# Loading an expert's rows one expert earlier, and spreading the gate's last steps over many blocks

## The chip, the cores and the metric

The kernel runs on one core of a Trainium2 chip. The core has the matrix engine TensorE (PE), the vector engine VectorE (DVE), ScalarE (ACT), GpSimd (POOL), SyncE (SP), which here mostly issues transfers, and 16 DMA engines. The metric is the device time of one execution in microseconds (us); smaller is better. TensorE runs at a clock that the chip grants: 1.00 in a row is the full 2.4 GHz, 0.50 is 1.2 GHz.

## What is computed

```python
def reference(**kw):
    attn_out = _attn_ref(...)                  # a scan over 768 steps, 4 x 8 heads of 40
    x = attn_out.transpose(0, 2, 1, 3).reshape(3072, 320)
    x = _moe_ref(x, w_gate, w1, w2, capacity)  # N, D, E, F = 3072, 320, 8, 1024
    return _moe2_ref(x, w_in, w_out)           # relu(x @ w_in)**2 @ w_out, width 2048

def _moe_ref(x, w_gate, w1, w2, capacity):
    logits = x @ w_gate
    expert_idx = np.argmax(logits, axis=1)
    gate_w = softmax(logits)[arange(N), expert_idx]
    ...                                        # row i goes to place counts[e] of its expert
    h = np.maximum(np.einsum('ecd,edf->ecf', disp, w1), 0.0)
    y = np.einsum('ecf,efd->ecd', h, w2)
    out[i] = gate_w[i] * y[expert_idx[i], pos[i]]   # for rows that had a place, else 0
```

All products are float32. The kernel splits an operand into a high part (rounded to TensorE's fp32r) and a low part (the rest) and adds three products: high by high, high by low, low by high.

## The kernel before

The program has three stages, one behind the other: the attention scan, which also computes the gate and scatters each token's row into a table of rows `zs_s` in memory; the **expert stage**, eight experts in an order that the gate decides at run time (largest count first); and the dense layer at the end ("moe2", tiles with a `g` at the end of their names), in six groups. The order of instructions on every engine is that of the code: the stage runs under a manual schedule, and nothing is reordered.

**An expert** has up to 480, 480, 480, 448, 416, 400, 384 and 384 rows in the order of experts. Its hidden width of 1024 is cut into eight **blocks** f = 0 to 7 (`Ffn.run`). A block does this, in this order:

- `first(f)`: 8 matmuls into `phe` (L1369), then ScalarE makes the high part of the activated block, `hhe` (L1373), and VectorE the low part, `hle` (L1374);
- `second(f-2)`: the block from two blocks earlier (`DEPTH = 2`) is multiplied into the outputs `poe`, three matmuls for each tile of rows (L1393 to L1395; four tiles of rows, three from expert 6 on). The third reads `hle`;
- `between(f)`, the work that is not the product itself. All of it is issued behind `second(f-2)`, and so VectorE meets it between the `hle` of this block and that of the next.

What `between` holds: **rows turned** at f = 2, 4 and 6 (4, 5, 6 for expert 0), each time a third of the next expert's rows, transposed by TensorE into `pte` (L1249) and split by ScalarE and VectorE (L1231, L1232, L1236, L1237); **weights** (`prep`), at each block the slices for a block up to four ahead, split by ScalarE (L1186, L1188, L1190), GpSimd (L1187) and VectorE (L1189, L1191), with a load of two slices by SP (L1165 to L1168); **`conv.step`**, which converts a piece of moe2's weights and stores it to memory (load L1090, ScalarE L1106, GpSimd L1107, VectorE L1108 to L1114, store L1115), at every block of experts 0 to 6 but the first four, and from expert 2 on but f = 4 and 6.

Three more pieces of the gate's arithmetic stand in it, each at one place: the rest of `gate.order` (24 short VectorE instructions) at f = 7 of expert 5; `gate.final` (the places of all tokens in the table, 30 VectorE instructions and a small matmul into `pfin`, L1030) at f = 7 of expert 6; and `places`, which makes one-hot matrices `oh` that put the last expert's rows straight into the first group of moe2, at f = 0 (two diagonals `Dslot`, `Dgate`, L1302, and some constants), f = 3 (three `oh`, L1316) and f = 5 (three pairs of L1322 and L1323) of expert 7.

The **row load** (L1491, `xs`, one DMA of 100 to 128 partitions, up to 1280 floats each) is issued by SP at the start of each expert, for the expert after it. Ahead of it SP reads that expert's number from `oat_i` into a register (L1448). `xs` has two buffers, and the rows of the running expert were turned in the expert before.

```python
                    nxt = load_next(e + 1) if e + 1 < NE else None      # before the blocks of e
                    ...
                        turns = (2, 4, 6) if e else (4, 5, 6)           # in between(f)
                        if f == turns[0] and nxt is not None:
                            st["x"] = F.xT(f"e{e + 1}", nxt)
                        if f in turns and nxt is not None:
                            next(st["x"])
```

Of the kernel before, what the change touches and what calls it, by code (L numbers as in the profile page):

```python
# [806 lines left out]
class Gate:  # L807
# [174 lines left out]
    def order(self, pool):  # L982
# [28 lines left out]
        for b in range(3):  # L1011
            V.memset(self.before[32 * b : 32 * b + 1, 32 * b + 32 :], 1.0)
        for i in range(n):
            V.memset(slots[:, i : i + 1], float(SLOTS[i + 1]))
            V.memset(base[:, i : i + 1], float(FROM[i + 1]))
        V.memset(self.base[:, 0:1], 0.0)
        V.memset(self.size[:, 0:1], float(SLOTS[0]))
# [4 lines left out]
        yield  # L1022

    def final(self, pool, ps):
        V, s2 = self.nc.vector, [128, NC]

        def t(shape, nm):
            return pool.tile(shape, F32, name=nm, bufs=1)

        self.nc.tensor.matmul(ps[:, 0:8], self.before, self.cntb, start=True, stop=True)  # L1030
        off = t([128, 8], "off")
        V.tensor_copy(off, ps[:, 0:8])
        q, pos, keep, big, a, b, bk, nb = (
            t([128, NC, 8] if n == "fq" else s2, n) for n in ("fq", "pos", "keep", "big", "fa", "fb", "bk", "nb"))
        V.tensor_tensor(q, self.oh, off.unsqueeze(1).to_broadcast([128, NC, 8]), ALU.mult)
        V.tensor_reduce(pos, q, axis=AX.X, op=ALU.add)
        V.tensor_tensor(pos, self.lp, pos, ALU.add)
        V.tensor_scalar(keep, pos, float(self.cap) - 0.5, None, ALU.is_lt)
        V.tensor_tensor(self.gate, self.gate, keep, ALU.mult)
        def of_token(z, out):  # L1040
            V.tensor_tensor(q, self.oh, z.unsqueeze(1).to_broadcast([128, NC, 8]), ALU.mult)
            V.tensor_reduce(out, q, axis=AX.X, op=ALU.add)

        of_token(self.size, big)
        V.tensor_tensor(big, self.ar, big, ALU.is_ge)
        of_token(self.base, a)
        V.tensor_tensor(a, a, self.ar, ALU.add)
        V.scalar_tensor_tensor(b, self.ei, float(self.capp), pos, ALU.mult, ALU.add)
        V.tensor_tensor(bk, big, keep, ALU.mult)
        V.tensor_scalar(nb, bk, -65536.0, 65536.0, ALU.mult, ALU.add)  # L1050
        V.tensor_tensor(nb, nb, b, ALU.add)
        V.tensor_copy(self.idxo, nb)

        V.tensor_scalar(nb, b, float(NE * NS1) - 0.5, float(FROM[NE]), ALU.is_gt, ALU.mult)
        V.tensor_tensor(b, b, nb, ALU.add)
        V.tensor_tensor(b, b, bk, ALU.mult)
        V.tensor_scalar(nb, big, -1.0, 1.0, ALU.mult, ALU.add)
        V.tensor_scalar_add(a, a, float(NE * NS1))
        V.tensor_tensor(a, a, nb, ALU.mult)
        self.slot = t([128, 4], "slot")  # L1060
        V.tensor_scalar_add(self.slot, a[:, 0:4], -float(NE * NS1 + FROM[NE - 1]))
        V.tensor_tensor(a, a, b, ALU.add)
        V.tensor_copy(self.idx, a)
        mc = t([128, 1], "mc")
        V.tensor_tensor(off, self.carA, self.size, ALU.subtract)
        V.tensor_reduce(mc, off, axis=AX.X, op=ALU.max)
        V.tensor_scalar(mc, mc, 0.5, None, ALU.is_gt)
        V.tensor_copy(self.ovf, mc)

# [124 lines left out]
class Ffn:  # L1194
# [90 lines left out]
    def places(self, slot, gate, nb, bs):  # L1285
# [24 lines left out]
        Ds, Dg = diag("slot", slot), diag("gate", gate)  # L1310
# [7 lines left out]
        yield  # L1318
# [5 lines left out]
        yield  # L1324
# [95 lines left out]
def tile_kernel(tc, cap, E, VN, VR, R0, R1, wg, w1, w2, wi, wo, out):  # L1420
# [32 lines left out]
    with ExitStack() as es0:  # L1453
# [26 lines left out]
        with ExitStack() as es:  # L1480
# [13 lines left out]
            def block(e):  # L1494
                return SLOTS[e] // -(-SLOTS[e] // 128)
# [49 lines left out]
            with tc.manual_schedule():  # L1545
                LEAD, done = 4, [4]

                def prep(s):

                    for _ in range(2):  # L1550
                        i = done[0]
                        if i > s + LEAD or i >= len(W):
                            break
                        if i % 2 == 0 and i >= 6:
                            W.load(i + 4, F.raw(f"rw{i + 4}"), 2)
                        W.prep(i)
                        done[0] += 1
# [8 lines left out]
                for i in range(3):  # L1566
                    conv.load(i)
                for e in range(NE):
                    X = F.X
                    F.busy = True  # L1570
                    nxt = load_next(e + 1) if e + 1 < NE else None
# [3 lines left out]
                    def between(f):  # L1575
                        turns = (2, 4, 6) if e else (4, 5, 6)
                        if f == turns[0] and nxt is not None:
                            st["x"] = F.xT(f"e{e + 1}", nxt)
# [5 lines left out]
                        if e == NE - 3 and f == 7:  # L1584
                            next(order)
                        if e == NE - 2 and f == 7:
                            gate.final(F.dp, F.ppt.tile([128, 512], F32, tag="t", name="pfin"))
                        if e == NE - 1:
                            if f == 0:
                                st["p"] = F.places(gate.slot, gate.gate, ns // bs, bs)  # L1590
# [4 lines left out]
                            if f in (0, 3, 5):  # L1595
                                next(st["p"])
# [9 lines left out]

                F.turn("g0", st["g"])
# [98 lines left out]
```

## Time and profile before

| | |
|---|---|
| median of 3 runs | 1069.04 us (1067.66 to 1071.59) |
| the profiled execution | 1070.31 us |
| its span, first to last instruction | 1068.60 us |
| mean granted clock over the span | 0.929 |
| TensorE busy (matmuls) | 952.2 us, 89% |
| VectorE busy | 689.8 us, 65% |
| ScalarE, GpSimd busy | 574.1 us, 341.7 us |
| the expert stage, from the trace | about 457 to 693 us |

Busy time is the time in which an engine executes an instruction. An engine carries out its instructions in the order written, so one that waits holds up everything behind it. The time outside the span (1070.31 - 1068.60 = 1.71 us) is start and end.

### The profile page before, as it was taken

To read this page: it belongs to the slowest core of one execution; us is meant where nothing else is said; L and a number is where in the kernel's file an instruction comes from. 1 tells how busy PE (TensorE), PEld (TensorE's weight loads), DVE (VectorE), ACT (ScalarE), POOL (GpSimd) and SP (SyncE) were. 2 spreads that over 40 slices of the span, in tenths; PEclk is the share of its full clock that TensorE was granted. 3 is DMA by queue.
4 is the path that set the end of the run, shared out by engine and by line. 5 is a ranking of instruction groups with operands and counts; after the bars stand their busy time and mean duration, and the time that the engine had idled before them with its cause. 6 is when DMAs were issued, how large, how long until landed. Compare 5 with 4: busy or idle time off the path is not lost.

```text
span 1068.6 us, 33405 instructions
## 1 busy us (share of the span) xinstructions
PE 952.2 (89%) x13866; PEld 865.0 (81%) x13866; DVE 689.8 (65%) x1407; ACT 574.1 (54%) x1344; POOL 341.7 (32%) x531
## 2 busy tenths in 40 slices
PE   5477887988879899998899999899999999999995
PEld 3366877877778788788799998788999999999995
DVE  6869678696776845568888888957434344444432
ACT  8245676766568688155556556456444443434331
POOL 5452454564554121126555555423201010000000
PEclk7587898988989899699899999999999999999998
DMA  7555665546543342267756776422200000000000
GB/s 185 128 139 168 187 190 170 150 142 177 145 124 99 94 118 78 86 185 217 222 166 217 227 231 205 140 75 78 62 14 25 25 26 25 1 25 1 25 1 29
DMA packets 80659, 122.89 MB, mean 115 GB/s; under 512 B 9679, under 2 KB 57409, under 8 KB 79561
## 3 DMA queue, kind: packets, MB, share of 16 engines
q1 hardware_dynamic: 71173, 100.09, 31.8%
q10 hardware_dynamic: 7020, 12.78, 4.2%
q0 software_dynamic: 2304, 7.78, 2.3%
q8 instruction: 111, 1.82, 0.7%
q14 instruction: 51, 0.42, 0.1%
HBM read 91.36 MB, written 29.35 MB: 113 GB/s over the span
## 4 chain that ended last, share of the span: by engine, by line
PE 61%; DVE 15%; DMA 7%; ACT 7%; issue 6%; POOL 2%; SPq 0%; ACTq 0%; DVEq 0%; POOLq 0%
PE phg L1369 14%; PE phe L1369 6%; PE pog L1395 5%; PE pog L1394 5%; PE pog L1393 5%; PE px L430 4%; PE pq L518 3%; DVE pr L287 2%; PE poe L1395 2%; DMA xs<-zs_s 2%; DMA wB<-in_E_dram 2%; PE poe L1393 2%; PE poe L1394 2%; PE pu L444 2%; PE py L540 1%
## 5 line engine op out<-in xcount | busy, mean ns | idle before, releaser
L1379 DVE SCALAR_TENSOR_TENSOR sqg<-phg,rg 128x512 f32<-128x512 f32 x96 | 66.3, 691 | 119.0 <-ACT rg L1378 119.0
L1378 ACT ACTIVATE rg<-phg 128x512 f32<-128x512 f32 x96 | 57.3, 596 | 110.4 <-PE phg L1369 110.2
L1381 DVE TENSOR_TENSOR hlg<-sqg,hhg 128x512 fp32r<-128x512 f32 x96 | 67.9, 707 | 65.9 <-ACT hhg L1380 63.2
L1380 ACT CAST hhg<-sqg 128x512 fp32r<-128x512 f32 x96 | 59.6, 620 | 79.0 <-DVE sqg L1379 79.0
L1369 PE MATMUL phg<-xhg,e 128*128 128x512 f32 x264 | 93.1, 393 | 0.0
L1395 PE MATMUL pog<-e,hlg 128*128 128x320 f32 x240 | 74.2, 309 | 0.0
L1394 PE MATMUL pog<-e,hhg 128*128 128x320 f32 x240 | 74.1, 309 | 0.0
L1393 PE MATMUL pog<-e,hhg 128*128 128x320 f32 x240 | 74.0, 308 | 0.0
L430 PE MATMUL px<-TB,X 128*104 128x128 f32 x384 | 64.7, 338 | 3.5 <-ACT TB L348 1.7
L1187 POOL TENSOR_TENSOR e<-rw,e 128x256 fp32r<-128x256 f32 x51 | 42.6, 840 | 71.0 <-ACT e L1186 60.2
L189 POOL TENSOR_TENSOR e<-e,wB 104x512 f32<-104x512 f32 x40 | 54.0, 1368 | 32.4 <-DVE wB L161 23.3
L430 PEld LDWEIGHTS px<-TB,X 128*104 128x104 f32 x384 | 58.8, 220 | 5.7 <-ACT TB L348 2.5
L189 POOL TENSOR_TENSOR e<-e 104x512 f32<-104x512 f32 x21 | 28.6, 1363 | 108.6 <-DVE e L165 49.0
L1508 POOL DMA_INDIRECT x2g<-zs_s,idx x24 | 23.7, 987 | 113.6 <-ACT hhg L1380 105.7
L1369 PE MATMUL phe<-xhe,e 128*128 128x480 f32 (+4 forms) x176 | 58.6, 374 | 0.0
L1369 PEld LDWEIGHTS phg<-xhg,e 128*128 128x128 f32 x264 | 49.6, 188 | 8.9
L518 PE MATMUL pq<-rq,vut 128*64 128x64 f32 x768 | 48.5, 232 | 8.0 <-ACT vut L509 7.8
L518 PEld LDWEIGHTS pq<-rq,vut 128*64 128x64 f32 x768 | 45.0, 144 | 11.0 <-ACT vut L509 10.6
L449 ACT COPY vu<-pu 32x320 f32<-32x320 f32 x96 | 40.0, 417 | 23.1 <-PE pu L444 21.7
L356 POOL COPY TB<-TT 32x256 f32<-32x256 f32 x92 | 42.6, 463 | 30.4 <-DVE TT L268 14.0
L1395 PE MATMUL poe<-e,hle 128*120 128x320 f32 (+4 forms) x150 | 47.5, 317 | 5.3 <-DVE hle L1374 5.3
L1373 ACT ACTIVATE hhe<-phe 128x480 fp32r<-128x480 f32 (+4 forms) x64 | 33.8, 529 | 34.0 <-PE phe L1369 33.7
(367 smaller groups left out, 2914.4 us busy)
## 6 DMA issues: line engine op xcount, KB each, us to landing
e<-in_E_dram ACTq DMA_DIRECT2D x60, 208.0 KB
rw<-in_w_dram SPq DMA_DIRECT2D x30, 320.0 KB
zs_s<-zt SPq DMA_DIRECT2D x24, 320.0 KB
rw<-in_w_dram SPq DMA_DIRECT2D x30, 256.0 KB
e<-in_E_dram SPq DMA_DIRECT2D x9, 832.0 KB
ru<-in_VR_dram SPq DMA_DIRECT2D x48, 128.0 KB
cr<-in_wi_dram SPq DMA_DIRECT2D x20, 256.0 KB
cr<-in_wo_dram SPq DMA_DIRECT2D x20, 256.0 KB
```

What stands on the lines that cost most here:

```text
L189: eng.tensor_tensor(z, z, f, ALU.mult)
L356: (copy or self.nc.gpsimd.tensor_copy)(self.TB[c % 2][t, :, t], self.TT[t, 8 * (c % 4) : 8 * (c % 4) + 8])
L430: self.nc.tensor.matmul(px[par][0:104, 128 * o : 128 * o + 128], X[:, par, o, :], TB[:, 4 * par + o, :], start=True, stop=True)
L518: T.matmul(pq[s, 64 * q : 64 * q + 64], vut[:, q, s], rt[:, :, q, pp], start=True, stop=True)
L1369: T.matmul(o, lt, rt, start=(i == 0), stop=(i == len(seq) - 1))
L1378: A.activation(r[:, :n], o, AF.Relu)
L1379: V.scalar_tensor_tensor(sq[:, :n], o, 0.0, r[:, :n], ALU.max, ALU.mult)
L1380: A.copy(hh[:, :n], sq[:, :n])
L1381: V.tensor_tensor(hl[:, :n], sq[:, :n], b32(hh)[:, :n], ALU.subtract)
L1393: T.matmul(o, hh[:, t], W["h2"], start=(f == 0), stop=False)
L1394: T.matmul(o, hh[:, t], W["l2"], start=False, stop=False)
L1395: T.matmul(o, hl[:, t], W["h2"], start=False, stop=(f == NF - 1))
```

## The change

Three things are moved; every instruction of before is still issued, and each engine has as many as it had.

1. **The row load** for expert e + 2 is issued at block 4 of expert e. The rows of expert 1 are loaded ahead of the loop, those of expert 2 at block 4 of expert 0.
2. **`gate.order`'s rest and `gate.final`** become one generator of 21 steps. A step of one to three short instructions is taken in each block of experts 2 to 6 in which no rows are turned, and the last is done in block 0 of expert 6.
3. **`places`** becomes a generator of more steps: the constants at block 7 of expert 6; then, in expert 7, `Dslot` at block 0, `Dgate` at 1, one `oh` each at 2, 3 and 4, and one pair for `gs` each at 5, 6 and 7.

```diff
@@ order
             V.memset(self.before[32 * b : 32 * b + 1, 32 * b + 32 :], 1.0)
+        yield
         for i in range(n):
             V.memset(slots[:, i : i + 1], float(SLOTS[i + 1]))
...
             V.tensor_reduce(to[:, 1:NE], cmp, axis=AX.X, op=ALU.add)
-        yield
+            yield
@@ final (a yield behind each one to three of its instructions)
-        self.nc.tensor.matmul(ps[:, 0:8], self.before, self.cntb, start=True, stop=True)
...
+        p = ps()
+        self.nc.tensor.matmul(p[:, 0:8], self.before, self.cntb, start=True, stop=True)
+        V.tensor_copy(off, p[:, 0:8])
+        yield
         V.tensor_tensor(q, self.oh, off.unsqueeze(1).to_broadcast([128, NC, 8]), ALU.mult)
+        yield
         V.tensor_reduce(pos, q, axis=AX.X, op=ALU.add)
+        yield
...
@@ places
-        Ds, Dg = diag("slot", slot), diag("gate", gate)
+        yield
+        Ds = diag("slot", gate.slot)
+        yield
+        Dg = diag("gate", gate.gate)
         yield
...
             self.oh.append(o)
-        yield
+            yield
...
             V.tensor_reduce(self.gs[:, i : i + 1], r, axis=AX.X, op=ALU.add)
-        yield
+            yield
@@ tile_kernel
+                def rest():
+                    yield from order
+                    yield from gate.final(F.dp, lambda: F.ppt.tile([128, 512], F32, tag="t", name="pfin"))
...
+                steps = rest()
+                nl = SLOTS[NE - 1]
+                spots = F.places(gate, -(-nl // 128), block(NE - 1))
+                ahead = {1: load_next(1)}
                 for e in range(NE):
...
-                    nxt = load_next(e + 1) if e + 1 < NE else None
+                    nxt = ahead.pop(e + 1, None)
...
+                        if f == 4 and e + 2 < NE:
+                            ahead[e + 2] = load_next(e + 2)
...
-                        if e == NE - 3 and f == 7:
-                            next(order)
                         if e == NE - 2 and f == 7:
-                            gate.final(F.dp, F.ppt.tile([128, 512], F32, tag="t", name="pfin"))
+                            next(spots)
+                        if 2 <= e < NE - 1 and f not in turns:
+                            next(steps, None)
                         if e == NE - 1:
-                            if f == 0:
-                                st["p"] = F.places(gate.slot, gate.gate, ns // bs, bs)
...
-                            if f in (0, 3, 5):
-                                next(st["p"])
+                            next(spots, None)
```

The order of instructions shows where they stand now. First SP, around the row load for expert 5 (400 rows: `xs` of 100 partitions); `rw` are weights, `cr` and `ct` the pieces of `conv.step`, `obe` the outputs of expert 3. Before, at the start of expert 4:

```order
L1090 DMA cr_10463<-in_wo_dram 128x512
L1115 DMA wof_s<-ct_10378 128x256
L1448 TENSOR_LOAD oat_i
L1448 ISA x2
L1491 ISA
L1491 DMA xs_10483<-zs_s 100x1280
L1165 ISA
L1165 DMA rw_10510<-in_w_dram 128x2x256
...
L1115 DMA wof_s<-ct_10465 128x256
L1402 DMA zs_s<-obe_0_10557 112x320
```

And with the change, in block 4 of expert 3 (the lines of after.py are some 20 higher):

```order
L1109 DMA cr_10333<-in_wo_dram 128x512
L1134 DMA wof_s<-ct_10293 128x256
L1470 TENSOR_LOAD oat_i
L1470 ISA x2
L1513 ISA
L1513 DMA xs_10379<-zs_s 100x1280
L1184 ISA
L1184 DMA rw_10388<-in_w_dram 128x2x256
...
L1134 DMA wof_s<-ct_10335 128x256
```

The load stands behind the conversion's store and ahead of a weight load as it did, half an expert earlier, and the first store behind it is that of the block after.

Next VectorE at the turn from expert 6 to expert 7. Before, all of `final` stands between two low parts:

```order
L1374 SCALAR_TENSOR_TENSOR hle_7_11599<-phe_7_11589,hhe_7_11598 128x384
L1189 TENSOR_TENSOR ws<-rw_11421,ws 64x128
L1191 TENSOR_TENSOR ws<-rw_11421,ws 128x320
L1032 COPY off<-pfin 128x8
L1035 TENSOR_TENSOR fq<-oh,off 128x192
L1036 TENSOR_REDUCE pos<-fq 128x24
L1037 TENSOR_TENSOR pos<-lp,pos 128x24
```

With the change the same instructions stand three experts earlier, one to three in a block:

```order
L1396 SCALAR_TENSOR_TENSOR hle_0_10134<-phe_0_10124,hhe_0_10133 128x448
L1208 TENSOR_TENSOR ws<-rw_9978,ws 64x128
L1210 TENSOR_TENSOR ws<-rw_9978,ws 128x320
L1127 TENSOR_SCALAR ct_10162<-ct_10162 128x256
L1128 SCALAR_TENSOR_TENSOR ct_10162<-cr_10020,ct_10162 128x256
L1132 TENSOR_SCALAR ct_10112<-ct_10112 128x256
L1133 SCALAR_TENSOR_TENSOR ct_10112<-cr_9916,ct_10112 128x256
L1041 COPY off<-pfin 128x8
L1396 SCALAR_TENSOR_TENSOR hle_1_10195<-phe_1_10185,hhe_1_10194 128x448
```

`off` is now made behind the conversion of block 0 of expert 3, and the next `hle` follows it at once.

## Rows read from the trace of the kernel before

**Rows 1.** The page, part 1: VectorE's busy time, share of the span, instructions.

```profile
PE 952.2 (89%) x13866; PEld 865.0 (81%) x13866; DVE 689.8 (65%) x1407; ACT 574.1 (54%) x1344; POOL 341.7 (32%) x531
```

**Rows 2.** Stretches, expert stage: from:to, length, busy (count) per engine, clock, DMA share, GB/s.

```profile
457.00:693.00 236.00, 218.88 (x1296) 207.77 (x1297) 195.74 (x451) 132.53 (x362) 120.48 (x149) 0.98 0.65 201
```

**Rows 3.** Waits of TensorE, 488.06 to 692.50 us: total, times, longest.

```profile
PE pte L1249 <- DMA xs<-zs_s: 11.5, 6, 4.1
PE poe L1395 <- DVE hle L1374: 5.3, 3, 4.6
```

**Rows 4.** Timeline of TensorE: start, length, instruction, [idle before it and its releaser].

```profile
528.57 0.98 PE L1249 MATMUL pte<-ident,xs 112*128 112x112 f32 x4 [4.09 <-DMA xs<-zs_s]
...
590.22 0.53 PE L1249 MATMUL pte<-ident,xs 100*128 100x100 f32 x4 [1.45 <-DMA xs<-zs_s]
...
674.24 0.63 PE L1395 MATMUL poe<-e,hle 128*128 128x320 f32 x1 [4.59 <-DVE hle L1374]
```

**Rows 5.** Stretches behind the two longest waits, and one at rest (PEclk is third from last).

```profile
528.57:534.50 5.93, 5.93 (x20) 5.36 (x21) 3.70 (x9) 3.25 (x9) 2.10 (x3) 0.52 1.03 338
534.50:540.00 5.50, 5.50 (x35) 5.13 (x34) 4.58 (x10) 1.83 (x5) 2.65 (x4) 1.00 0.67 214
674.24:677.50 3.26, 3.26 (x11) 3.26 (x12) 3.08 (x14) 0.00 (x0) 2.65 (x3) 0.50 0.27 71
```

**Rows 6.** Stretches from an expert's first `hle`: experts 1 and 6, and 1 to 6.

```profile
488.06:521.87 33.81, 30.68 (x180) 28.36 (x180) 28.32 (x61) 18.44 (x51) 19.36 (x25) 1.00 0.69 216
...
643.21:673.63 30.42, 24.77 (x153) 23.50 (x151) 27.20 (x76) 16.95 (x50) 14.75 (x18) 1.00 0.66 208
...
488.06:673.63 185.57, 169.12 (x1017) 161.45 (x1016) 155.22 (x365) 105.41 (x290) 99.82 (x124) 0.98 0.68 212
```

**Rows 7.** Waits of VectorE, 488.06 to 673.63 us.

```profile
DVE ct L1108 <- POOL ct L1107: 9.3, 6, 2.2
DVE e L1189 <- ACT e L1188: 3.7, 3, 1.3
DVE ws L1189 <- ACT ws L1188: 3.7, 3, 1.3
DVE xle L1232 <- ACT xhe L1231: 2.9, 4, 0.9
DVE xRle L1237 <- ACT xRhe L1236: 1.5, 1, 1.5
```

**Rows 8.** Timeline of VectorE, 640 to 680 us.

```profile
665.80 0.16 DVE L1032 COPY off<-pfin 128x8 f32<-128x8 f32 x1
...
671.42 0.78 DVE L1057 TENSOR_SCALAR nb<-big 128x24 f32<-128x24 f32 x1
...
673.63 0.55 DVE L1374 SCALAR_TENSOR_TENSOR hle<-phe,hhe 128x384 fp32r<-128x384 f32 x1
...
674.98 0.17 DVE L1291 MEMSET ones<- 128x128 f32 x1
...
676.61 0.86 DVE L1302 TENSOR_SCALAR Dslot<-ident,slot 128x128 f32<-128x128 f32 x4
```

**Rows 9.** Timelines of SP's queue, ScalarE and VectorE, start of expert 4.

```profile
585.03 0.35 SPq L1491 DMA_DIRECT2D xs<-zs_s  x1
...
588.64 0.37 SPq L1115 DMA_DIRECT2D wof_s<-ct  x1
...
593.85 0.43 ACT L1106 ACTIVATE ct<-cr 128x256 f32<-128x256 f32 x1 [1.71 <-DMA wof_s<-ct]
...
595.25 0.29 DVE L1108 TENSOR_SCALAR ct<-ct 128x256 int32<-128x256 int32 x1 [2.17 <-POOL ct L1107]
```

**Rows 10.** Stretches: behind a row load, and around block 4 of the same expert.

```profile
590.00:596.00 6.00, 5.78 (x37) 5.76 (x38) 3.35 (x8) 3.05 (x9) 1.74 (x3) 1.00 0.88 269
602.00:608.00 6.00, 6.00 (x41) 5.95 (x40) 4.78 (x10) 2.83 (x7) 1.58 (x2) 1.00 0.64 209
```

**Rows 11.** A stretch of the attention scan with many short idle times of TensorE.

```profile
294.00:321.00 27.00, 21.48 (x638) 19.49 (x635) 20.27 (x30) 17.75 (x44) 14.69 (x19) 0.87 0.41 127
```

More of the change, by code (lines that the diff above doesn't have):

```diff
@@ L1012, in order @@
             V.memset(self.before[32 * b : 32 * b + 1, 32 * b + 32 :], 1.0)
+        yield
         for i in range(n):
             V.memset(slots[:, i : i + 1], float(SLOTS[i + 1]))
+        V.memset(self.size[:, 0:1], float(SLOTS[0]))
+        yield
+        for i in range(n):
             V.memset(base[:, i : i + 1], float(FROM[i + 1]))
         V.memset(self.base[:, 0:1], 0.0)
-        V.memset(self.size[:, 0:1], float(SLOTS[0]))
+        yield
         for z, to in ((slots, self.size), (base, self.base)):
@@ L1039, in final @@
         V.tensor_tensor(self.gate, self.gate, keep, ALU.mult)
[L1040 to L1044, printed above, removed]
+        yield
+        V.tensor_tensor(q, self.oh, self.size.unsqueeze(1).to_broadcast([128, NC, 8]), ALU.mult)
+        yield
+        V.tensor_reduce(big, q, axis=AX.X, op=ALU.add)
         V.tensor_tensor(big, self.ar, big, ALU.is_ge)
-        of_token(self.base, a)
+        yield
+        V.tensor_tensor(q, self.oh, self.base.unsqueeze(1).to_broadcast([128, NC, 8]), ALU.mult)
+        yield
+        V.tensor_reduce(a, q, axis=AX.X, op=ALU.add)
         V.tensor_tensor(a, a, self.ar, ALU.add)
+        yield
         V.scalar_tensor_tensor(b, self.ei, float(self.capp), pos, ALU.mult, ALU.add)
@@ L1050, in final @@
         V.tensor_scalar(nb, bk, -65536.0, 65536.0, ALU.mult, ALU.add)
+        yield
         V.tensor_tensor(nb, nb, b, ALU.add)
         V.tensor_copy(self.idxo, nb)
+        yield
         V.tensor_scalar(nb, b, float(NE * NS1) - 0.5, float(FROM[NE]), ALU.is_gt, ALU.mult)
         V.tensor_tensor(b, b, nb, ALU.add)
+        yield
         V.tensor_tensor(b, b, bk, ALU.mult)
@@ L1058, in final @@
         V.tensor_scalar_add(a, a, float(NE * NS1))
+        yield
         V.tensor_tensor(a, a, nb, ALU.mult)
-        self.slot = t([128, 4], "slot")
         V.tensor_scalar_add(self.slot, a[:, 0:4], -float(NE * NS1 + FROM[NE - 1]))
+        yield
         V.tensor_tensor(a, a, b, ALU.add)
         V.tensor_copy(self.idx, a)
-        mc = t([128, 1], "mc")
+        yield
         V.tensor_tensor(off, self.carA, self.size, ALU.subtract)
         V.tensor_reduce(mc, off, axis=AX.X, op=ALU.max)
+        yield
         V.tensor_scalar(mc, mc, 0.5, None, ALU.is_gt)
         V.tensor_copy(self.ovf, mc)
+        yield
 class Conv:
@@ L1283, in xT_sum, with places @@
             self.halves(X, k, ps[k], slice(0, n))
-    def places(self, slot, gate, nb, bs):
+    def places(self, gate, nb, bs):
         V, A, T = self.nc.vector, self.nc.scalar, self.nc.tensor
@@ L1308, in spread @@
             return p
-        Ds, Dg = diag("slot", slot), diag("gate", gate)
+        yield
+        Ds = diag("slot", gate.slot)
+        yield
+        Dg = diag("gate", gate.gate)
         yield
@@ L1317, in places @@
             self.oh.append(o)
-        yield
+            yield
         p = spread("gate", Dg)
@@ L1323, in places @@
             V.tensor_reduce(self.gs[:, i : i + 1], r, axis=AX.X, op=ALU.add)
-        yield
+            yield
     def turn(self, nm, t):
@@ L1605, in tile_kernel @@
                             pass
+                for _ in spots:
+                    pass
                 F.turn("g0", st["g"])
```

3 lines of the change are left out of this document (2 added, 1 removed).

## Prediction

> **What bounds the kernel now.** I begin with the page: TensorE is the busiest engine and VectorE stands at 65% [rows 1]. That share is a mean over three stages, and the change touches one. So I look at the stretch of the expert stage alone: there TensorE is busy 218.9 of 236 us and VectorE 195.7 [rows 2], 83%. The next view is TensorE's waits in this stage. There are two that count: 11.5 us for the row loads, once in each of six experts (4.1 at most), and 5.3 us for VectorE's `hle`, of which one single wait is 4.6 [rows 3]. The timeline says where: 4.09 us ahead of the first turn at 528.57, shorter ones such as 1.45 us at 590.22, and 4.59 us at 674.24 [rows 4]. Then the clock: behind the 4.09 us the granted clock was 0.52 for 5.93 us, behind the 4.59 us it was 0.50 for 3.26 us, and soon after the first it was 1.00 again [rows 5]. Half of such a stretch is lost: 5.93 x 0.48 = 2.8 us and 3.26 x 0.50 = 1.6 us.
>
> If TensorE were the only limit, all of this would come back. So I ask how VectorE stands, and for that I cut the stage where VectorE does the first `hle` of an expert. From that of expert 1 (488.06) to that of expert 7 (673.63) there are 185.57 us, and VectorE is busy in 155.2 of them, 84%; in expert 6 it is 27.20 of 30.42 [rows 6]. That reads like room. But the waits of VectorE in the same stretch add up to 9.3 + 3.7 + 3.7 + 2.9 + 1.5 = 21.1 us only [rows 7]. The other 185.6 - 21.1 = 164.5 us it was at work: 155.2 busy and 9.3 in short gaps between its 365 instructions, 0.03 us each, which have no releaser. Now the same for TensorE: 185.6 less 11.5 (rows), 0.7 (`hle`, the short waits: 5.3 - 4.6), 4.0 (the part of the 4.59 us that lies ahead of 673.63) and 2.8 (clock) is 166.6 us of work. **The two engines have the same amount to do**, 166.6 and 164.5 us, and today each waits some 20 us. This decides the case: what TensorE stops waiting for, it gains only as far as VectorE follows.
>
> **The row load.** Six waits, 11.5 us, and the slow clock behind the longest, 2.8 us. The load takes about 5 us: issued at 585.03 [rows 9], used at 590.22 [rows 4]. Issued at block 4 it has until block 2 of the next expert, six blocks of 30.4 / 8 = 3.8 us [rows 6], 23 us. Even four times its time would be hidden, so I price these waits at zero. Where does it go? Into a calmer place: behind a row load the DMA engines were 0.88 busy, around block 4 only 0.64 [rows 10]. From expert 2 on no conversion step is in block 4, so no store of a step is queued right behind the load. Every issue counts: SP issues the same transfers, only in another order, and the weights queued behind the load at block 4 serve a block up to four ahead, 15 us; the load's 5 us fits in that. At zero; if that cover is gone, a wait for weights of up to 5 us in each of six experts.
>
> **What VectorE gets from it.** ScalarE works in order, and it stood behind the late turn; behind that, its conversion step waited 1.71 us more for a store that was issued 3.6 us after the row load, and through GpSimd this reached VectorE as 2.17 us [rows 9]. There are six of these, 9.3 us, and the waits for the split of the turned rows, 2.9 + 1.5 us, hang on the same place. These 13.7 us could all stay (upper end) or all go (zero). With the load elsewhere and no late turn, what is left should be the store's own time, so I take a value near the lower end: 1.5 us. The waits of the weights' low part on ScalarE, 3.7 + 3.7 us, lie behind the last turn of an expert, where ScalarE makes two copies of its third; nothing there is changed, and they stay: 7.4 us.
>
> **`final` and `order`, spread.** `final` is a lump on VectorE from 665.80 to 673.63, 7.8 us in which no `hle` can be made; that is what TensorE's 4.59 us waited for. The 30 instructions are still executed; their time lies inside the 164.5 us, since they move from one part of the stretch to another. In blocks of experts 2 to 6 they come one to three at a time, at most 0.8 us each [rows 8], so no later `hle` is late by more than about 1 us by them. Nothing is saved in VectorE's sum. The clock's 1.6 us behind the lump go away with it.
>
> **`places`.** Its constants, 674.98 to 676.61, 1.6 us [rows 8], move from behind the first `hle` of expert 7 to ahead of it. They add 1.6 us to VectorE's stretch. The one-hot steps are now one in a block; the last pair for `gs` falls in block 7, ahead of the end of the last products, which it does not hold up as long as it is done within a block; its two instructions are on 128x512, where the `hle` of 128x384 took 0.55 us [rows 8], so the cost is at most 1.5 us. I take zero.
>
> **The sum.** VectorE's stretch: 164.5 + 1.6 + 7.4 + 1.5 = 175.0 us against 185.6, so 10.6 us less; with 1.6 us of clock in expert 7, 12.2 us. The profiled execution would go from 1070.31 to 1058.1. It lies 1.27 us above the median of the runs, so I forecast 1057 us for the median, 1.1% less. TensorE would lose its row waits and get new ones: 175.0 - 166.6 = 8.4 us for `hle`, in many small pieces.
>
> **Rivals.**
>
> A. *VectorE follows all the way, TensorE is the bound.* For it speaks that VectorE's busy share of 84% looks like a reserve of 30 us. Then the stretch is TensorE's 166.6 us, 19.0 less, and with 1.6 us it is 20.6: 1049.7 for the execution, 1048.5 for the median. Against it: the gaps are part of the work, and VectorE's own 164.5 + 1.6 + 7.4 are above 166.6. For this VectorE's 7.4 us on ScalarE would have to shrink as well. The Trainium skill has a rule that speaks for it: "Perfetto Trace Analysis", section Identifying the Most-Contended Engine, takes occupancy as a fair measure of how near VectorE is to its limit; by that rule it would be 16% away from it here, which would lead to this rival. The trace does not agree, as I read it: of the 30.4 idle us 9.3 are gaps between instructions.
>
> B. *VectorE's waits on the conversion stay.* If the store is slow by itself and not because of the row load, most of the 13.7 us remain. With half of them, 6.9, the stretch is 180.4: 5.2 + 1.6 = 6.8 us gained, 1062.2 for the median. With all of them it is 164.5 + 1.6 + 21.1 = 187.2, 1.6 us longer than before, and with the clock's 1.6 us the time is that of before. For it: the same store would still be followed by a step on one shared SP queue. Against it: each of these waits was found behind a late turn.
>
> C. *The clock, and slower.* VectorE-bound, TensorE no longer waits in six long pieces but for a moment in most blocks. Its clock was 0.87 in a stretch of the scan where it was busy for 21.5 of 27 us in short pieces [rows 11]. With the expert stage at 0.87 TensorE would need 166.6 / 0.87 = 191.5 us, 5.9 more than the 185.6, and nothing would come back in expert 7: 1076.2, median 1075. Slower than before begins below 166.6 / 185.6 = 0.90. Against it: with its short waits for `hle` in expert 6 the clock stayed at 1.00 in that whole stretch [rows 6]. The Trainium skill speaks for it: "TensorE: Matmul & The Clock Gate", section A second HAM failure mode: psum-queue depth-cycling, describes a kernel in which many small idle times between groups of matmuls made the clock swing; the 0.87 of the scan agrees, expert 6 does not.
>
> D. *The change does not do what it says*: a row load still late. It would need to take over 20 us where 5 were seen. Then only the lump's wait and its clock come back, 4.6 + 1.6 = 6.2 us: 1064.1 for the execution, 1062.8 for the median; 1 in 100.
>
> **How the numbers follow.** My forecast, 1053 to 1061, has a chance of 62%; A (1047 to 1053) 12%; B 18%, one half of it at 1061 to 1063.5 and one half from there to 1070; C and D together 5%; the other 3% is something that I do not see, on either side. Ends of the range: 1052 at the bottom leaves out most of A; 1063 at the top takes in the better half of B. What it leaves out is about 10% below and 12% above. A measurement of this kernel can tell about 0.5%, 5.3 us, from no change, so faster means below 1063.7: 62 + 12 + 9 and a little, 84%. Same: the rest of B and some of the unknown, 12%. Slower, above 1074.4: 4%, mostly C.
>
> **What would show it.** In the profile after: no wait of TensorE on `xs`; none over 2 us on `hle`; the granted clock 1.00 around the first turn of expert 2 and the start of expert 7; VectorE's stretch from the first `hle` of expert 1 to that of expert 7 near 175 us with about 10 us of waits in it, mostly behind the third part of the turn; TensorE's waits for `hle` 7 to 9 us in all. It is wrong if VectorE still waits some 9 us for the conversion at block 2 (B), if TensorE shows hardly any wait on `hle` (A), or if the clock falls below 0.95 in the expert stage (C). A step not seen here would show as a new line in TensorE's waits: for `pslot` or `pgate` in expert 7, or for weights behind block 4.

## The result, and the profile after

| | before | after |
|---|---|---|
| median of 15 runs each | 1070.88 us (1067.66 to 1078.82) | 1060.52 us (1055.42 to 1066.13) |
| profiled execution | 1070.31 us | 1060.98 us |
| span | 1068.60 us | 1059.20 us |

The ratio is 0.989, with a 95% interval of 0.9866 to 0.9915: 1.1% faster. The forecast was 1057 against a median of 1069.04, which is 0.9887.

The page shows hardly anything of it (its columns as in [rows 1]):

```profile
PE 950.9 (90%) x13866; PEld 862.4 (81%) x13866; DVE 693.5 (65%) x1407; ACT 572.4 (54%) x1344; POOL 340.9 (32%) x531
```

The stretches do. These are, in the changed kernel, the stretch from the first `hle` of expert 1 to that of expert 7, the start of expert 7, and all that lies ahead of expert 1 (columns as in [rows 2]):

```profile
490.79:664.03 173.24, 167.18 (x1011) 158.02 (x1011) 156.40 (x373) 101.31 (x284) 98.02 (x121) 1.00 0.70 218
664.03:690.00 25.97, 23.93 (x150) 22.26 (x149) 22.40 (x46) 12.11 (x34) 10.74 (x12) 1.00 0.49 145
0.00:490.79 490.79, 403.54 (x10715) 360.56 (x10716) 350.75 (x746) 301.50 (x735) 201.23 (x367) 0.86 0.51 143
```

The first answers to 185.57 us in [rows 6]: 12.3 us less, and the granted clock is 1.00 in it and behind it, where it was 0.52 and 0.50 in two places [rows 5]. What lies ahead of expert 1 is the same work in both kernels but for the place of the row loads; it took 2.7 us longer in this execution than in the one of before (490.79 against 488.06). This part wanders, and by more than that, between the profiled executions (last section). So traces are compared here from the first `hle` of expert 1 to the end: 1068.60 - 488.06 = 580.54 us before, 1059.20 - 490.79 = 568.41 after, **12.1 us less**; 12.2 were forecast. The parts agree less well than the total: 12.3 us less in the stretch where 10.6 were forecast, and 0.2 us more from expert 7 on where 1.6 less were forecast.

TensorE's waits in the stretch, and the one in expert 7 behind it (columns as in [rows 3]):

```profile
PE poe L1417 <- DVE hle L1396: 5.0, 8, 1.3
PE pte L1268 <- DVE off L1041: 0.9, 1, 0.9
...
PE pslot L1326 <- DVE Dslot L1321: 2.0, 1, 2.0
```

The 11.5 us on `xs` are gone. In their place stand 5.9 us on VectorE in the stretch, in nine small waits, and one of 2.0 us behind it. VectorE's own waits in the stretch are two of the five groups of [rows 7], as long as they were, and a rest of a third:

```profile
DVE e L1208 <- ACT e L1207: 3.7, 3, 1.3
DVE ws L1208 <- ACT ws L1207: 3.7, 3, 1.3
DVE ct L1127 <- POOL ct L1126: 1.5, 2, 0.7
```

So VectorE waits 8.9 us where it waited 21.1, and is at work for the other 164.3 us: 12.2 us of its waits are gone from a stretch that is 12.3 us shorter. TensorE's waits and slow clock have shrunk by about as much, so this alone does not tell which of the two engines decides.

### The profile page after: what moved, and what is told of

Same layout as the page of the kernel before. It is cut to its first block, busy times and chain, and to the rows that moved or that the text cites. A ratio compares the mean times of both kernels' runs of the same rounds, so it can differ in the third digit from the quotient of the medians.

```text
span 1059.2 us, 33405 instructions
## 1 busy us (share of the span) xinstructions
PE 950.9 (90%) x13866; PEld 862.4 (81%) x13866; DVE 693.5 (65%) x1407; ACT 572.4 (54%) x1344; POOL 340.9 (32%) x531
## 4 chain that ended last, share of the span: by engine, by line
PE 61%; DVE 16%; DMA 7%; issue 6%; ACT 6%; POOL 2%; SPq 0%; ACTq 0%; DVEq 0%; POOLq 0%
PE phg L1391 16%; PE pog L1417 5%; PE pog L1416 5%; PE pog L1415 5%; PE phe L1391 4%; PE px L430 4%; DVE pr L287 3%; PE pq L518 3%; DMA wB<-in_E_dram 2%; PE pu L444 2%; PE poe L1417 1%; PE py L540 1%; PE poe L1415 1%; PE poe L1416 1%; DMA e<-in_E_dram 1%
## 5 line engine op out<-in xcount | busy, mean ns | idle before, releaser
L430 PE MATMUL px<-TB,X 128*104 128x128 f32 x384 | 67.5, 348 | 6.8 <-issue 4.4
L430 PEld LDWEIGHTS px<-TB,X 128*104 128x104 f32 x384 | 61.3, 228 | 9.0 <-issue 4.9
L1391 PE MATMUL phg<-xlg,e 128*128 128x512 f32 x132 | 51.8, 392 | 0.0
L356 POOL COPY TB<-TT 32x256 f32<-32x256 f32 x92 | 41.4, 450 | 31.0 <-DVE TT L268 14.2
```

The source lines that it names most:

```text
L430: self.nc.tensor.matmul(px[par][0:104, 128 * o : 128 * o + 128], X[:, par, o, :], TB[:, 4 * par + o, :], start=True, stop=True)
L1391: T.matmul(o, lt, rt, start=(i == 0), stop=(i == len(seq) - 1))
```

## The experiments

Two theories. **V**: VectorE sets the pace of the expert stage, and the late rows cost time because VectorE, too, stood idle behind them. **T**: TensorE sets the pace, and what comes back are its own waits, 11.5 + 2.8 us for the rows and 4.6 + 1.6 us for the lump of `final`. All in one table; the ratio is to the kernel before, on the same chip; the stretch is that from the first `hle` of expert 1 to that of expert 7, and "to the end" runs from the former to the end of the span. The two last columns are of one execution of each kernel. In the fourteen traces the part from expert 7's first `hle` to the end took 393.5 to 396.7 us, so a difference of one or two us "to the end" is weak evidence.

| kernel | ratio (95%) | stretch, us | to the end, us |
|---|---|---|---|
| before | 1 | 185.57 | 580.54 |
| whole change | 0.989 (0.9866 to 0.9915) | 173.24 | 568.41 |
| rows_only | 0.9856 (0.9813 to 0.99) | 171.93 | 566.39 |
| spread_only | 0.9969 (0.9941 to 0.9996) | 182.89 | 576.52 |
| rows_start | 0.9923 (0.9894 to 0.9952) | 178.38 | 575.06 |
| places_lump | 0.9872 (0.9833 to 0.9911) | 169.92 | 566.23 |
| v_plus | 1.0115 (1.0067 to 1.0163) | 196.21 | 592.87 |
| p_plus | 0.9897 (0.9859 to 0.9936) | 175.00 | 569.97 |
| v_minus | 0.9861 (0.9814 to 0.9907) | 170.52 | 564.03 |
| r_pool | 1.0022 (0.9995 to 1.0048) | 185.44 | 579.00 |
| rows_swap | 0.9872 (0.983 to 0.9913) | 171.68 | 566.14 |
| full_prep | 0.9885 (0.9839 to 0.9931) | 175.29 | 569.25 |
| rows_prep | 0.9874 (0.983 to 0.9918) | 172.63 | 568.24 |
| lump_prep | 0.9903 (0.9869 to 0.9937) | 173.83 | 570.40 |

### The two halves apart: rows_only and spread_only

```diff
 # rows_only: before.py with
+                ahead = {1: load_next(1)}
-                    nxt = load_next(e + 1) if e + 1 < NE else None
+                    nxt = ahead.pop(e + 1, None)
+                        if f == 4 and e + 2 < NE:
+                            ahead[e + 2] = load_next(e + 2)
```

> The kernel before with the early row load alone; order, final and places stand in their lumps as before. Theory V (VectorE sets the pace of the expert stage; the late rows cost because VectorE stood idle behind them): the lump costs VectorE the same wherever it stands, so the stretch from the first hle of expert 1 to that of expert 7 is 164.5 + 7.4 + 1.5 = 173.4 us or some 2 us more, against 176.5 with the whole change, and the kernel is as fast as with the whole change or up to 3 us faster: 0.985 to 0.990 of before, though TensorE still waits 4 us or more for the lump. Theory T (TensorE sets the pace, and what comes back are its own waits): the rows are 14.3 of the 20.5 us of waits and slow clock, 70% of the gain: 0.992 of before, and 3.5 to 6 us above the whole change.

The waits of the early row load alone: TensorE's in the stretch and the one at the lump of `final`, then VectorE's in the stretch.

```profile
PE poe L1395 <- DVE hle L1374: 1.1, 3, 0.5
...
PE poe L1395 <- DVE hle L1374: 5.1, 1, 5.1
```

```profile
DVE e L1189 <- ACT e L1188: 3.7, 3, 1.3
DVE ws L1189 <- ACT ws L1188: 3.7, 3, 1.3
DVE ct L1108 <- POOL ct L1107: 2.9, 3, 1.4
```

The lump stands, TensorE waits 5.1 us for it, more than before, and still the kernel is 14.2 us shorter to the end than before, 2.0 us shorter than with the whole change. A wait of TensorE that leaves the time as it was is what V expects: TensorE waits there for the engine that is behind, and removing the wait does not make that engine faster. T's 0.992 lies outside the interval. (The 176.5 us that the expectation gives for the whole change, and the one for r_pool below, is not its stretch, which took 173.24 us.)

```diff
 # spread_only: after.py with
-                ahead = {1: load_next(1)}
-                    nxt = ahead.pop(e + 1, None)
+                    nxt = load_next(e + 1) if e + 1 < NE else None
-                        if f == 4 and e + 2 < NE:
-                            ahead[e + 2] = load_next(e + 2)
```

> The changed kernel with the row load back at the start of each expert. Theory V: VectorE has as much to do as before, plus 1.6 us for the constants of places and about 2.5 us because single steps beside GpSimd take longer (0.89 us for a product that took 0.35 in the lump); it still stands idle behind late rows for some 8 to 14 us. The time is that of before: 0.997 to 1.003. Theory T: the lump's wait and its slow clock, 6.2 of 20.5 us, go: 0.994 to 0.997.

```profile
PE pte L1268 <- DMA xs<-zs_s: 12.0, 5, 4.0
...
DVE ct L1127 <- POOL ct L1126: 8.0, 6, 1.5
```

The ratio, 0.9969, lies at the edge of both ranges, so the time alone does not decide. The trace, with TensorE's and VectorE's longest waits above, tells what the 4.0 us to the end are. 2.7 lie in the stretch: VectorE's waits are 8.0 + 3.7 + 3.7 + 1.3 + 0.9 = 17.6 us instead of 21.1, since steps now stand where it was idle behind late rows. The other 1.3 lie behind it; the 1.6 us of slow clock that go with the lump would fit, but that part differs by up to 3.2 us among the traces, so this is not shown. Added to the early row load, which takes that idle time away, the spreading of `order`, `final` and `places` together brings nothing: in the traces rows_only is 2.0 us shorter than the whole change, and by the times, whose intervals overlap, it is no slower.

### Does VectorE set the pace: v_plus, v_minus, p_plus

```diff
 # v_plus: after.py with
-        V.tensor_tensor(W["l2"], r2, b32(W["h2"]), ALU.subtract)
+        for _ in range(2 if 4 <= i < 64 else 1):
+            V.tensor_tensor(W["l2"], r2, b32(W["h2"]), ALU.subtract)
```

> The changed kernel with the low part of w2 (128x320, 0.52 us on VectorE) made twice for every slice of the expert stage from the fifth on, 48 more instructions in the stretch from the first hle of expert 1 to that of expert 7. Theory V: VectorE has no room; the stretch of 173.2 us grows by 48 x 0.55 = 26 us, and the time goes to about 1.013 of before. Theory T: 15% of VectorE's time is free, which is 26 us; the time grows by 5 us at most and stays below 0.995 of before.

The stretch, and TensorE's longest waits in it:

```profile
479.63:675.84 196.21, 173.42 (x1011) 159.02 (x1009) 180.45 (x420) 102.35 (x285) 98.56 (x122) 0.99 0.63 192
...
PE poe L1418 <- DVE hle L1397: 13.9, 20, 1.6
PE phe L1392 <- ACT xRle L1258: 6.9, 6, 2.0
```

VectorE's busy time went up by 180.45 - 156.40 = 24.1 us, the stretch by 23.0. VectorE was busy for only 156.4 of 173.2 us, and the other 16.8 us (T's expectation put them at 26) were not free: with them free, 24.1 us more would have lengthened the stretch by some 7 us. Of the 16.8, 8.9 are its waits and 7.9 gaps between instructions. Only the 1.5 us of waits for the conversion took up added work: 7.4 us of waits are left. T's 5 us are refuted.

```diff
 # v_minus: after.py with, for 4 <= i < 64,
-        V.tensor_tensor(W["l2"], r2, b32(W["h2"]), ALU.subtract)
+        A.copy(W["l2"], r2)
```

> The changed kernel with VectorE's subtraction for the low part of w2 left out in the expert stage, where ScalarE writes a plain copy in its place (so the products of the low part are not those wanted). Theory V: VectorE has 48 x 0.55 = 26 us less to do, more than it lacks; TensorE becomes the bound, its 5.9 us of waits on VectorE in the stretch and the 2.0 for the diagonal go: a stretch of 167 to 169 us and 0.981 to 0.985 of before. Theory T: no change from the whole change, 0.987 to 0.991. If ScalarE's 48 copies (0.46 us each, 22 us) delay its own steps, a part is lost.

The stretch, TensorE's longest wait and VectorE's:

```profile
488.17:658.69 170.52, 164.86 (x1004) 156.94 (x1003) 136.49 (x324) 116.85 (x330) 97.17 (x121) 1.00 0.73 222
...
PE poe L1420 <- DVE hle L1399: 3.8, 6, 1.1
...
DVE ct L1127 <- POOL ct L1126: 18.2, 23, 2.2
```

VectorE is busy for 19.9 us less, and this brought 2.7 us in the stretch, less than the 4 to 6 us that V expected, and 4.4 to the end. The ratio, 0.9861, lies between the two expectations, and its interval takes in both. Taking work off VectorE soon meets a second limit: TensorE is busy for 164.9 of the 170.5 us, and VectorE now waits 18.2 us for GpSimd's part of the conversion.

```diff
 # p_plus: after.py, Ffn.first with
+        if not square:
+            T.matmul(o, *seq[0], start=True, stop=True)
```

> The changed kernel with the first matmul of every block of the expert stage done twice: 64 more of 128 x 384 to 480 columns, 0.18 to 0.22 us each by their distance in the trace, 12.6 us in all, 9.6 of it in the stretch. Theory V: TensorE's 7.9 us of waits on VectorE swallow most of it: 3 to 7 us above the whole change, 0.992 to 0.996 of before. Theory T: all of it shows, 12 us, 1.000 or more.

```profile
486.73:661.73 175.00, 173.58 (x1062) 167.67 (x1061) 156.72 (x373) 103.92 (x284) 97.45 (x121) 1.00 0.71 215
...
PE poe L1419 <- DVE hle L1398: 1.4, 2, 0.9
```

Above, the stretch and TensorE's only wait in it. The added matmuls cost less than the 9.6 us that were priced: TensorE's busy time in the stretch rose by 173.58 - 167.18 = 6.4 us. Of these 4.5 came out of its waits there (5.9 us in the changed kernel, 1.4 now) and 1.8 show in the stretch; to the end it is 1.6, less than V expected. So 24 us more on VectorE showed almost in full, and 6.4 us more on TensorE by little over a quarter. This settles the order: VectorE first, TensorE close behind it.

### Where the row load stands: rows_start

```diff
 # rows_start: after.py with the load for e + 2 ahead of the blocks of e
+                    if e + 2 < NE:
+                        ahead[e + 2] = load_next(e + 2)
-                        if f == 4 and e + 2 < NE:
-                            ahead[e + 2] = load_next(e + 2)
```

> The changed kernel with the load of the rows of expert e + 2 at the start of expert e, where before the rows of e + 1 were loaded: an expert ahead, but just in front of the same store of the conversion as before. If VectorE's waits for the conversion (9.3 us before, 1.5 after) came from the late turn alone, they stay below 2.5 us and the time is that of the change, 0.987 to 0.991. If the load delayed the store, most of the 9.3 us are back and the time is 0.994 or more.

Timelines of SP's queue, ScalarE and VectorE at the start of expert 2:

```profile
514.06 0.38 SPq L1513 DMA_DIRECT2D xs<-zs_s  x1
...
517.75 0.37 SPq L1134 DMA_DIRECT2D wif_s<-ct  x1
...
522.69 0.44 ACT L1125 ACTIVATE ct<-cr 128x256 f32<-128x256 f32 x1 [5.65 <-DMA wif_s<-ct]
...
524.09 0.29 DVE L1127 TENSOR_SCALAR ct<-ct 128x256 int32<-128x256 int32 x1 [2.04 <-POOL ct L1126]
```

No row is late here, and still ScalarE waits 5.65 us for a store of the conversion issued 3.7 us after the row load, and VectorE behind it. VectorE's waits for the conversion add up to 7.2 us; the stretch is 5.1 us longer than with the load at block 4. So it is both: the early load alone does not give the whole gain, and 5.1 of the 12.3 us in the stretch hang on its place. ScalarE could go on only 4.9 us after the store's issue (517.75 to 522.69). Whether the store was held up by its place in SP's queue or by what else the DMA engines had to move, no run separates. The ratio, 0.9923, lies between the two expectations.

### Places as before: places_lump

```diff
 # places_lump: after.py with places in three steps again
-                        if e == NE - 2 and f == 7:
-                            next(spots)
-                            next(spots, None)
+                            if f in (0, 3, 5):
+                                next(spots)
 # ... (and the yields inside places are those of before.py again)
```

> The changed kernel with places as it was: everything up to the diagonals at block 0 of expert 7, three one-hot matrices at block 3, three pairs at block 5. Theory V: VectorE's constants move back, 1.6 us less in its stretch; in expert 7 TensorE needs the slot diagonal at block 3 instead of block 2, so the 2.0 us wait for it goes. From the first hle of expert 1 to the end 0 to 3.5 us less than the whole change: 0.985 to 0.989. Theory T: the spread of places took a wait away, and without it the time is 0 to 2 us longer: 0.989 to 0.991.

The stretch, TensorE's waits in it, and VectorE's:

```profile
487.27:657.19 169.92, 164.84 (x999) 155.97 (x999) 153.99 (x365) 99.72 (x279) 96.93 (x121) 1.00 0.73 220
...
PE poe L1414 <- DVE hle L1393: 4.1, 8, 1.3
PE pte L1268 <- DVE off L1041: 0.9, 1, 0.9
...
DVE e L1208 <- ACT e L1207: 3.7, 3, 1.3
DVE ws L1208 <- ACT ws L1207: 3.7, 3, 1.3
DVE ct L1127 <- POOL ct L1126: 0.7, 1, 0.7
```

The wait for the slot diagonal is gone; the stretch is 3.3 us shorter and the time to the end 2.2 us, within V's range. Of the 3.3 us, 1.6 to 1.9 are the constants, which only change sides: the part from expert 7's first `hle` to the end is 1.1 us longer. The ratio's interval overlaps that of the whole change, so the time alone does not tell the two apart.

This kernel is also rows_only with nothing but `order` and `final` spread. The two take the same time to the end (566.23 and 566.39 us), and VectorE is at work in the stretch for 161.8 us and 161.6 (its length less its waits). So in these traces the spreading of `order` and `final` costs as much as it brings, and the 2.0 us by which the whole change is longer than rows_only lie with the spreading of `places`.

### Ways past the limit that failed: r_pool, rows_swap, and the three with block 6 turned round

```diff
 # r_pool: after.py with
-        V.tensor_tensor(W["R"][64:128], rR[64:128], b32(W["R"])[64:128], ALU.subtract)
+        (V if own or i >= 64 else self.nc.gpsimd).tensor_tensor(W["R"][64:128], ...)
```

> The changed kernel with the low part of the weights' third part (64x128, on VectorE 48 times in the stretch at 0.39 us on average, and the 7.4 us of waits for ScalarE in front of it) on GpSimd in the expert stage. Theory V: VectorE has some 20 + 7 us less to do, TensorE becomes the bound, and the stretch of 176.5 us loses TensorE's waits on VectorE, 5.9 us: 0.982 to 0.986 of before; no wait of TensorE on hle is left. Theory T (VectorE is not the limit now): no change, 0.988 to 0.991. If the longer work of GpSimd slows VectorE or its own steps of the conversion, a part of it is lost.

Stretch and VectorE's longest wait:

```profile
486.00:671.44 185.44, 169.68 (x997) 156.74 (x996) 136.87 (x324) 100.12 (x279) 128.20 (x170) 0.99 0.66 203
...
DVE ct L1127 <- POOL ct L1126: 33.9, 31, 1.3
```

VectorE is busy for 19.5 us less and loses all of it, and more, waiting for GpSimd, which makes the conversion's next input only after the weights. V's forecast missed: work taken off the limiting engine was put ahead of what that engine waits for.

```diff
 # rows_swap: rows_only, Conv.step with the piece of the step before first
+            V.tensor_scalar(u, u, 1, None, ALU.logical_shift_right)
+            V.scalar_tensor_tensor(u, s, -0x80000000, u, ALU.bitwise_and, ALU.bitwise_or)
 # ...
             V.tensor_scalar(t, m.bitcast(I32), 0x08000000, 4, ...)
             V.scalar_tensor_tensor(t, lo, 28, t, ...)
 # ... (the same pair for u behind these two goes)
```

> The early row load alone, and in each step of the conversion VectorE finishes the piece of the step before ahead of starting the new one (the two pairs of instructions swapped). Now the last of the four takes 0.85 us where the same form takes 0.43 as the second; in the trace it lies beside GpSimd's addition that starts when the second is done. If the two disturb each other, swapped they do not meet (the addition then lies beside the next hle, which reads TensorE's result): 36 x 0.43 = 15 us less for VectorE in the stretch, and TensorE binds: 4 to 7 us below the run with the early row load alone, 0.979 to 0.982 of before. If another instruction gets longer by the same amount instead, no change.

VectorE's groups (line, operation, count | busy us, mean ns | idle), first of rows_only, then of rows_swap:

```profile
L1114 DVE SCALAR_TENSOR_TENSOR ct<-cr,ct 128x256 int32<-128x256 int32 x38 | 32.4, 853 | 1.3
...
L1191 DVE TENSOR_TENSOR e<-rw,e 128x320 fp32r<-128x320 f32 x30 | 15.9, 532 | 0.9
```

```profile
L1196 DVE TENSOR_TENSOR e<-rw,e 128x320 fp32r<-128x320 f32 x30 | 21.6, 719 | 0.9
...
L1111 DVE SCALAR_TENSOR_TENSOR ct<-cr,ct 128x256 int32<-128x256 int32 x36 | 15.3, 425 | 1.2
```

The instruction meant got as short as hoped, 425 ns instead of 853, and others longer instead: the low part of w2 719 instead of 532. The stretch is the same, 171.68 against 171.93. The second expectation held: the price moved to other instructions of VectorE. One of them is the low part of w2 at 524.50 in rows_swap, which took 0.92 us beside GpSimd's split of weights (524.27 to 525.07).

```diff
 # full_prep, rows_prep, lump_prep: weights ahead of the third part of the turn,
 # in after.py, rows_only and places_lump
-                        if f in turns and nxt is not None:
+                        if f in turns[:2] and nxt is not None:
                             next(st["x"])
                         prep(8 * e + f)
+                        if f == turns[2] and nxt is not None:
+                            next(st["x"])
```

> The changed kernel with the weights' part of block 6 put ahead of the third part of the turn (before it, ScalarE copies the turned rows first, and VectorE waits 1.2 us for the weights behind them, 7.4 us in six experts). Theory V: removing a wait of VectorE helps although TensorE never waited for it directly: VectorE's stretch loses up to 7.4 us, TensorE's waits for it (5.9 us in the stretch, 2.0 behind) shrink to about 1, and the time is 4 to 7 us below the whole change: 0.983 to 0.986 of before. Theory T: no change, 0.988 to 0.991.

> The early row load alone, with the same swap in block 6. Theory V: VectorE's stretch loses up to 7.4 us, but TensorE, with 1.3 us of waits in it, has no more to give there; only the 5.1 us at the lump of final get shorter as far as VectorE is ahead: 0 to 5 us below the early row load alone, 0.981 to 0.986 of before. The lump should now be the one wait left, and here the spread would pay. Theory T: no change, 0.985 to 0.987, with the lump's wait of 5 us.

> The changed kernel with places as before and the same swap in block 6: the candidate for the fastest. Theory V: TensorE's 4.1 us of waits on hle in the stretch go, 3 to 5 us below the run with places as before: 0.982 to 0.985 of before. Theory T: no change, 0.987.

Waits of TensorE, then of VectorE, in the stretch of full_prep:

```profile
PE phe L1391 <- ACT xRle L1257: 6.1, 6, 1.3
PE poe L1417 <- DVE hle L1396: 3.1, 5, 1.2
```

```profile
DVE hle L1396 <- ACT hhe L1395: 5.7, 5, 1.2
DVE ct L1127 <- POOL ct L1126: 3.7, 3, 2.0
```

VectorE's 7.4 us for the weights are gone, and 5.7 us for `hhe` took their place, in all three kernels; its waits in the stretch of full_prep are 9.4 us, 8.9 in the changed kernel. Here the turned third came later as well, and TensorE waits 6.1 us for it at the start of each expert (6.5 in lump_prep, 0.6 in rows_prep). All three were 0.8 to 4.2 us longer to the end than the kernels they came from. V's gain did not come: the wait that was removed came back as another. Of the kernels that compute the wanted result, none is clearly faster than the early row load alone, and that one is told from the whole change by 2.0 us in one execution of each, not by the intervals of the times.

## Why the prediction was right, by its own steps

**The bound.** That VectorE and TensorE have nearly the same amount to do, and that VectorE decides, held: v_plus, p_plus and rows_only show it. Rival A, that VectorE's busy share means room, is refuted by v_plus. Rival D went as well: no wait on `xs` is left.

**The row load.** Its waits were priced at zero, which was right. The new place was chosen as "calmer" and priced at zero, which was right too, and rows_start shows that 5.1 of the 12.3 us hang on it. I had taken VectorE's waits behind the turn down from 13.7 to 1.5 us mostly because the turn was no longer late; they did fall to 1.5, but with the load at the start of an expert those for the conversion were 7.2 without any late turn. Rival B's mechanism exists; the change steps around it, which the prediction gave only as one reason of two.

**VectorE's sum.** 175.0 us forecast, 173.24 measured. The waits are those of the forecast, 7.4 and 1.5. The work came out as 164.3 instead of 166.1, and this hides two errors that go against each other. The first is that the instructions moved were taken to be as long as they were, single ones at most 0.8 us: spread, they got longer. The 56 instructions of `order` (26 of them, not 24) and `final` in the stretch, count times mean of each group added up, took 11.0 us in two lumps and 15.1 us spread. In the changed kernel, VectorE and then GpSimd at one of them:

```profile
558.36 0.90 DVE L1043 TENSOR_TENSOR fq<-oh,off 128x192 f32<-128x192 f32 x1
...
566.29 0.34 DVE L1045 TENSOR_REDUCE pos<-fq 128x24 f32<-128x192 f32 x1
```

```profile
557.43 0.73 POOL L1137 TENSOR_TENSOR ct<-ct,one 128x256 int32<-128x256 int32 x1 [0.97 <-PE phe L1391]
558.11 0.93 POOL L1206 TENSOR_TENSOR ws<-rw,ws 128x256 fp32r<-128x256 f32 x1
```

The product took 0.90 us beside GpSimd's work on weights. In the lump the same one took 0.70 us with a GpSimd instruction beside its start, and the two products of the same shape, with next to none beside them, took 0.35 each. The reduction, 0.34, is as long as it was there. GpSimd is busy for 98.0 of the 173.2 us of the stretch, and was for 3.3 of the 7.8 us of the lump of `final`. The longer durations, 4.1 us, were taken at nothing. The Trainium skill's page "SBUF — State Buffer", section SBUF: two separate sides, describes one pair of ports that VectorE's instructions with two inputs in SBUF and GpSimd's take in turn, each for a whole instruction; the product, which got longer, and the swapped conversion agree with it. The second error makes up for it: what is left of VectorE's work is some 6 us shorter than in the trace of before (164.3 - 1.6 - 15.1 = 147.6 against 164.5 - 11.0 = 153.5). Of this 2.1 us are a shorter 64x128 subtraction (21.0 us in 48 before, 18.9 in 48 after), 0.8 the 128x320 one, and 1.4 shorter gaps (9.3 against 7.9); one more `hle` in the stretch, 0.6 us, goes the other way. Another 2.3 are no gain at all: records of neighbouring instructions overlap, so that the durations add up to 10.8 us more than the busy time before and 13.1 after. So the 4.1 us are not time lost, and places_lump against rows_only, 161.8 and 161.6 us of work, says the same of `order` and `final`: "nothing is saved" stands. Why the rest got shorter, no run shows.

**Expert 7.** The 1.6 us of clock did not show: from its first `hle` to the end it took 394.97 us before and 395.17 after. The slow clock did go, and a wait of 2.0 us for the slot diagonal came; but this part differs by up to 3.2 us among the traces, so the two cannot be set against each other in the total. `places` was taken at zero past the 1.6 us of constants, which left this wait out, though `pslot` was named as one to look for. In the changed kernel, VectorE and then GpSimd:

```profile
665.68 2.36 DVE L1321 TENSOR_SCALAR Dslot<-ident,slot 128x128 f32<-128x128 f32 x4
```

```profile
665.87 0.73 POOL L1206 TENSOR_TENSOR ws<-rw,ws 128x256 fp32r<-128x256 f32 x1 [0.76 <-ACT ws L1205]
666.54 1.16 POOL L1527 MEMSET x2g<- 128x1280 f32 x1
```

The same four instructions took 0.86 us in [rows 8]. Now they lie beside GpSimd's split and the clearing of the gathered rows, and the block in which TensorE wants them is one earlier. The price hangs on what GpSimd does at that moment: spread_only, with `places` in the same steps, has `Dslot` in 1.36 us and no wait for it, and in places_lump `Dslot` took 0.86 us and `Dgate`, which then lay beside the same two, 2.32, with no wait of TensorE on it. These are the two diagonals of places_lump:

```profile
660.17 0.86 DVE L1321 TENSOR_SCALAR Dslot<-ident,slot 128x128 f32<-128x128 f32 x4
660.95 2.32 DVE L1321 TENSOR_SCALAR Dgate<-ident,gate 128x128 f32<-128x128 f32 x4
```

What the wait costs in time is not shown: the 2.2 us that places_lump gains to the end lie ahead of expert 7, and its part from expert 7 on is the longer one.

**TensorE's waits** in the stretch were forecast at 8.4 us in many small pieces; they are 5.9 in nine, with the stretch 1.7 us shorter than forecast. Rival C is refuted: the mean clock is 1.00 over the stretch and the start of expert 7.

**The total.** The mechanism was right. That 12.1 us came out where 12.2 were forecast is in part luck: 1.7 us more than forecast in the stretch make up for the 1.6 us that did not come in expert 7.

## What to carry to other kernels

Whether an engine has room is read from what its idle time is released by, not from its busy share: in the changed kernel VectorE was full at 90% busy (156.4 of 173.2 us). The engine that shows the waits need not be the one that decides; give each of the two some extra work, and see which one's work shows in the time. A transfer moved earlier wants a place where nothing that is waited for stands close behind it. Work spread out of a lump runs beside other engines' work that it did not meet in the lump, and its instructions can get longer.

## What the runs showed of the hardware that was not expected

The part ahead of expert 1, with the same 10715 matmuls in each kernel, took 488.06 us before, 490.79 after, and 477.96 in rows_prep, at a mean granted clock of 0.86, 0.86 and 0.89. In rows_prep:

```profile
0.00:477.96 477.96, 389.94 (x10715) 347.84 (x10716) 353.62 (x746) 300.27 (x735) 203.43 (x367) 0.89 0.54 147
```

The difference is as large as the whole effect of the change, so spans of single executions are not compared here. Each kernel was profiled once, so how much the stretch behind it varies from one execution to the next is not known.

Behind the 5.1 us at the lump of rows_only the clock was 0.53 for 3.3 us, as in [rows 5]; behind the 2.0 us for the diagonal it stayed at 1.00. With that wait and that clock rows_only was still 2.0 us shorter to the end, in one execution of each, than the whole change, which has neither.
